# Scores turned by VectorE for batches 2 to 7, low parts of the weights by GpSimd, a new order of the first block, and four output tiles at the end

## The chip, the core and the metric

The kernel runs on one core of a Trainium2 chip. Its time is the device time of one execution in microseconds (us). A profile of another execution gives the start and length of every instruction. TensorE (PE) multiplies, VectorE (DVE) and ScalarE (ACT) work on whole tiles, GpSimd (POOL) is a fourth engine, and SyncE (SP) here only issues DMAs. Every engine works through its own queue in order and waits on semaphores for the others.

## What is computed

Attention over 8 batches, 8 heads, 576 positions and 64 columns a head, and behind it a gated layer on the 4608 x 512 result:

```python
mask_local = (rel >= 0) & (rel < stride)                      # heads 0 to 3, stride = 32
mask_strided = (rel >= 0) & (pos[None, :] % stride == pos[:, None] % stride)   # heads 4 to 7
scores = np.where(masks, scale * q @ k.T, -1e9)
attn = softmax(scores) @ v                                    # -> x, 4608 x 512
gate = 1.0 / (1.0 + np.exp(-(x @ w_gate)))                    # 512 x 1536
out = (gate * (x @ w_val)) @ w_out                            # 1536 x 512
```

## The kernel before

**The gated layer.** The 512 first positions of each batch make one block of 512 tokens (blocks 0 to 7); the 64 left over of every batch make block 8. A block goes through 12 slices of the 1536 columns. A slice f has three groups of 12 TensorE products of 128 x 512: the gate (PSUM bank `g`), the value (bank `v`) and the output, which adds to four banks in two tiles `o0` and `o1`. Twelve, because every 32-bit factor is split into a rounded high part and a low part, and three products replace one: `xh` and `xl` for the tokens, two halves of `w` for the weights, `hh` and `hl` for the hidden values. After the gate, ScalarE computes `t` and `e`; VectorE makes `e`, `t` and `hl` of them and of `v`, ScalarE `hh`. The output group of a slice comes one slice later (`last`). At a block's end the four output banks are copied to tiles `ob`, the even ones by ScalarE (buffer `ost`) and the odd ones by VectorE (buffer `l0`), and a DMA takes each out. The banks of the next block's output are free when the copies are done.

**Attention** goes by pairs of heads: steps 0 and 2 of a batch are local, 1 and 3 strided. For each pair: Q and V load, Z sets padding to zero (GpSimd), S computes scores as small products (`s`), F adds the mask and subtracts the maximum (VectorE), E takes the exponential (ScalarE), N normalises (VectorE), T turns the result with TensorE transposes into PSUM (`t`), P copies it back to SBUF (`pt`, ScalarE), X weighs the values (`x`, products of 64 x 64 array tiles), H and L split the result into `xh` and `xl`, R keeps the left-over positions. One PSUM tile of two banks, tag `a`, serves s, t and x in turn.

**Order.** In blocks 1 to 6, while block k is computed, the attention of batch k + 1 is strewn between its groups: `block` calls the next piece of the generator `attention` after the groups in `AT`, numbered 0 to 8 over three slices. For these blocks TensorE's order is the program's, and the order of the other engines is left to a scheduler. The first block, with the attention of batches 0 and 1 and the preparation of the weights, follows the string `ORDER`, for all engines: a token such as `X13` is step X of batch 1, pair 3; `W3.0` loads weight 0 of slice 3, `a`, `b` (ScalarE), `w` (VectorE), `u` (ScalarE) and `l` (VectorE) make its high and low parts; `g`, `s`, `m`, `x`, `y` and `O` are the parts of the gated layer.

Of the kernel before, what the change touches and what calls it, by code (L numbers as in the profile page):

```python
# [62 lines left out]
w1.2 g1.0.3 g1.1.3 g0.1.3 a2.2 g2.0 m0 u1.2 b2.2 l1.2 s1 W3.1 w2.2 x0 g2.1 a3.0 y0 u2.2 m1 b3.0 l2.2 s2 W3.2
w3.0 x1 O0 a3.1 y1 u3.0 m2 b3.1 l3.0 W4.0 S10 x2 w3.1 a3.2 O1 Z10 F10 Q11 u3.1 b3.2 W4.1 a4.0 w3.2 g3.0 E10
l3.1 y2 b4.0 N10 g3.1 a4.1 W4.2 u3.2 s3 l3.2 w4.0 O2 b4.1 m3 a4.2 W5.0 w4.1 x3 b4.2 T10 y3 u4.0 W5.1 w4.2 O3
P10 l4.0 u4.2 a5.0 l4.2 u4.1 g4.0 b5.0 l4.1 W5.2 w5.0 a5.1 b5.1 u5.0 g4.1 W6.0 w5.1 s4 l5.0 u5.1 l5.1 a5.2
g5.0 b5.2 m4 W6.1 w5.2 x4 a6.0 y4 u5.2 X10 b6.0 l5.2 s5 W6.2 w6.0 a6.1 O4 V11 b6.1 u6.0 W7.0 w6.1 H10 g5.1
# [14 lines left out]
def attention_then_glu(ctx, tc, qk_l, qk_s, v_l, v_s, w_all, consts, out):  # L82
# [75 lines left out]
    def lower(f, i):  # L158
        a, _ = words.pop((f, i))
        nc.vector.tensor_tensor(wl[f][i], a.bitcast(F32), wh[f][i].bitcast(F32), op=ALU.subtract)  # L160

    def pair(b, step, space):
# [88 lines left out]

        def spread():
            tp = todo["spread"]
            tiles["pt"] = pt = space.tile([P, 2 * SS * QB], F32, tag="pt", name=f"pt{b}_{step}")
            n = len(pairs) * P
            for lo, hi in ((0, BANK), (BANK, n)):
                if hi > lo:
                    nc.scalar.copy(pt[:, lo:hi], tp[:, lo:hi])  # L258
            if ns % 2:
                nc.scalar.copy(pt[:QB, n : n + P], tp[:QB, n : n + P])  # L260
# [331 lines left out]
```

## Time and profile before

| | |
|---|---|
| median of 3 runs | 1027.22 us (1026.4 to 1027.34) |
| profiled execution | 1023.94 us, span 1022.1 us |
| mean granted TensorE clock | 0.987 |
| instructions | 18250 |
| HBM read, written | 55.42 MB, 9.44 MB |

The span is the time from the first to the last instruction. A row of a group reads: line, engine, operation, what is written and from what, shape and number; behind the bar its busy us, the mean ns of one, and the idle time of the engine just before it, with what ended that. A row of a timeline reads: start in us from the span's beginning, length in us, engine, line, operation, shape and number of equal ones. PE is TensorE's products and PEld its weight loads, which overlap. A 32-bit small product shows as two entries.

### The profile page before, as it was taken

Reading aid. Unit: us, or ns where it says so; the run is one execution under the profiler, and the core shown is the slowest. Engines: PE = TensorE matmul, PEld = TensorE weight load, DVE = VectorE, ACT = ScalarE, POOL = GpSimd, SP = SyncE. Lnnn points to the kernel's source line nnn. Section 1 sums busy time; section 2 is a strip of 40 time slices with the busy share of each in tenths; the row PEclk is TensorE's granted clock in tenths of the full one; section 3 lists DMA queues with packets and bytes.
Section 4 is the critical chain, followed back from the end, with each engine's and each line's share of the span. In section 5 each row is a group of like instructions: output and inputs, shape, how many; then the busy total and the mean of one; then the engine's idle time right before and its main releaser. Section 6 shows DMA issues by size and latency. Waiting matters only on the chain.

```text
span 1022.1 us, 18250 instructions
## 1 busy us (share of the span) xinstructions
PE 995.9 (97%) x7984; PEld 812.5 (79%) x7984; DVE 491.3 (48%) x850; ACT 340.4 (33%) x683; POOL 3.4 (0%) x20
## 2 busy tenths in 40 slices
PE   4999999999999999999999999999999999999996
PEld 4787778888888888888888888888888888888885
DVE  6788864444444454444544454444444533333322
ACT  4787853322222232222222222223222322222221
POOL 0000000000000000000000000000000000000000
PEclk7899999999999999999999999999999999999999
DMA  7666632110211121101211021112110010001001
GB/s 256 210 178 214 210 97 79 51 41 28 89 40 51 40 77 55 51 22 45 82 50 37 29 91 41 51 40 71 61 51 17 1 42 1 1 0 42 1 1 42
DMA packets 19872, 66.04 MB, mean 65 GB/s; under 512 B 2256, under 2 KB 2384, under 8 KB 19792
## 3 DMA queue, kind: packets, MB, share of 16 engines
q1 hardware_dynamic: 18352, 59.28, 17.9%
q10 hardware_dynamic: 1440, 5.59, 1.7%
q8 instruction: 63, 1.03, 0.4%
q14 instruction: 17, 0.14, 0.0%
HBM read 55.42 MB, written 9.44 MB: 63 GB/s over the span
## 4 chain that ended last, share of the span: by engine, by line
PE 91%; DMA 3%; DVE 3%; ACT 2%; issue 0%; SPq 0%; ACTq 0%; DVEq 0%
PE v L359 28%; PE o L413 27%; PE g L359 27%; PE x L276 4%; PE s L206 3%; DMA raw<-in_w_all 2%; PE t L245 2%; ACT high L137 1%; PE gv L359 1%; ACT low L141 0%; DMA qk<-in_qk_l 0%; DVE high L147 0%; PE t L249 0%; DVE w L160 0%; ACT pt L258 0%
## 5 line engine op out<-in xcount | busy, mean ns | idle before, releaser
L413 PE MATMUL o<-w,hh 128*128 128x512 f32 x864 | 269.1, 393 | 0.0
L359 PE MATMUL v<-xh,w 128*128 128x512 f32 x784 | 264.8, 398 | 0.0
L359 PE MATMUL g<-xh,w 128*128 128x512 f32 x784 | 259.1, 391 | 0.0
L413 PEld LDWEIGHTS o<-w,hh 128*128 128x128 f32 x864 | 160.1, 188 | 33.3
L376 DVE TENSOR_SCALAR t<-t 128x512 int32<-128x512 int32 x96 | 41.0, 427 | 281.6 <-ACT t L373 281.6
L359 PEld LDWEIGHTS v<-xh,w 128*128 128x128 f32 x784 | 147.6, 188 | 33.1
L359 PEld LDWEIGHTS g<-xh,w 128*128 128x128 f32 x784 | 147.5, 188 | 31.0 <-issue 0.2
L413 PE MATMUL o<-w,hl 128*128 128x512 f32 x432 | 168.3, 389 | 0.0
L373 ACT ACTIVATE t<-g 128x512 f32<-128x512 f32 x96 | 57.4, 598 | 314.5 <-PE g L359 314.5
L359 PE MATMUL v<-xl,w 128*128 128x512 f32 x392 | 153.6, 392 | 0.0
L359 PE MATMUL g<-xl,w 128*128 128x512 f32 x392 | 152.8, 390 | 0.0
L400 DVE SCALAR_TENSOR_TENSOR e<-e,v 128x512 f32<-128x512 f32 x96 | 66.0, 687 | 125.5 <-PE v L359 125.5
L392 ACT ACTIVATE hh<-t 128x512 fp32r<-128x512 f32 x108 | 68.3, 632 | 148.6 <-DVE t L401 145.6
L395 DVE SCALAR_TENSOR_TENSOR hl<-t,hh 128x512 fp32r<-128x512 f32 x108 | 74.7, 691 | 48.5 <-ACT hh L392 48.5
L413 PEld LDWEIGHTS o<-w,hl 128*128 128x128 f32 x432 | 81.1, 188 | 17.4 <-DVE hl L395 0.2
L359 PEld LDWEIGHTS g<-xl,w 128*128 128x128 f32 x392 | 73.9, 188 | 15.2
L359 PEld LDWEIGHTS v<-xl,w 128*128 128x128 f32 x392 | 73.9, 189 | 13.8
L401 DVE SCALAR_TENSOR_TENSOR t<-t,e 128x512 f32<-128x512 f32 x96 | 66.4, 692 | 3.3
L374 ACT ACTIVATE e<-g 128x512 f32<-128x512 f32 x96 | 57.1, 595 | 0.0
L276 PEld LDWEIGHTS x<-pt,vv 64*64 64x64 f32 (+1 forms) x1856 | 37.0, 142 | 13.7 <-issue 9.3
L230 ACT ACTIVATE sb<-sb 128x640 f32<-128x640 f32 (+1 forms) x32 | 23.8, 745 | 70.4 <-DVE sb L226 70.4
L276 PE MATMUL x<-pt,vv 64*64 64x32 f32 (+1 forms) x1856 | 40.9, 230 | 3.3 <-DVE xl L311 1.4
(59 smaller groups left out, 675.4 us busy)
## 6 DMA issues: line engine op xcount, KB each, us to landing
raw<-in_w_all SPq DMA_DIRECT2D x36, 512.0 KB, 3.8
qk<-in_qk_s SPq DMA_DIRECT2D x14, 599.0 KB, 3.9
vv<-in_v_l SPq DMA_DIRECT2D x13, 640.0 KB, 4.1
qk<-in_qk_l SPq DMA_DIRECT2D x14, 592.0 KB, 4.0
out<-ob SPq DMA_DIRECT2D x32, 256.0 KB, 2.0
vv<-in_v_s SPq DMA_DIRECT2D x13, 384.0 KB, 3.2
vv<-in_v_l ACTq DMA_DIRECT2D x3, 640.0 KB, 5.8
qk<-in_qk_s ACTq DMA_DIRECT2D x2, 599.0 KB, 4.7
```

The lines of the kernel that those rows point to most:

```text
L206: nc.tensor.matmul(sc[g * m : (g + 1) * m, j * BANK + s * kk : j * BANK + (s + 1) * kk], qk[d, q0 : q0 + m], qk[d, k0 : k0 + kk], start=Tr ...
L230: nc.scalar.activation(prob, prob, AF.Exp, scale=SCALE)
L276: nc.tensor.matmul(xp[j * D : (j + 1) * D, r * BANK + (u * per + g) * m : r * BANK + (u * per + g + 1) * m], v[rows, (u * per + g) * P + j ...
L359: nc.tensor.matmul(o, w, x, start=first and n == 0, stop=last and n == len(todo) - 1)
L373: nc.scalar.activation(t, g, AF.Tanh, scale=0.5)
L374: nc.scalar.activation(e, g, AF.Exp)
L376: nc.vector.tensor_scalar(ti, ti, 0x7FFFFFFF, None, op0=ALU.bitwise_and)
L392: nc.scalar.activation(hh, t, AF.Copy, scale=half)
L395: nc.vector.scalar_tensor_tensor(hl, t, half, hh.bitcast(F32), op0=ALU.mult, op1=ALU.subtract)
L400: nc.vector.scalar_tensor_tensor(e, e, 1.0, v, op0=ALU.min, op1=ALU.mult)
L401: nc.vector.scalar_tensor_tensor(t, t, 1.0, e, op0=ALU.add, op1=ALU.mult)
L413: nc.tensor.matmul(acc[k][i], h[:, i * P : (i + 1) * P], w, start=f == 0 and n == 0, stop=f == NF - 1 and n == 2,)
```

## The change

- For batches 2 to 7 the steps T and P fall away. In their place stands `turn_blocks`: eight VectorE instructions a pair, each transposing the 32 x 32 blocks of 32 partitions. The values and the strided classes are laid out otherwise on the host for these batches (`by_batch`, `FEW`, `MOST`), so that the weighing finds its rows; `weigh` takes half as many groups in a row from one half of the partitions (`per`) before it goes to the other half.
- A pair now has two pieces instead of three, at slots 0 and 7 instead of 0, 4 and 6.
- `lower`, the low part of each of the 36 weights, goes from VectorE to GpSimd.
- `ORDER` is another order of the same steps.
- In block 8 the four output tiles have four buffers (`ost`, `l0`, `t`, `e`) instead of two.

```diff
+BY_PE = 2
-AT = (0, 4, 6)
+AT = (0, 7)
 ORDER = """
...
-y10 l11.1 X13 s11 a11.2 g11.1 H13 b11.2 L13 R13 w11.2 O10 m11 u11.2 l11.2 x11 y11
+l11.1 a11.2 T13 b11.2 g11.1 P13 w11.2 u11.2 l11.2 X13 m11 x11 R13 y11 H13 L13
...
+FEW, MOST = slice(0, BY_PE), slice(BY_PE, B)
...
     def lower(f, i):
         a, _ = words.pop((f, i))
-        nc.vector.tensor_tensor(wl[f][i], a.bitcast(F32), wh[f][i].bitcast(F32), op=ALU.subtract)
+        nc.gpsimd.tensor_tensor(wl[f][i], a.bitcast(F32), wh[f][i].bitcast(F32), op=ALU.subtract)
...
+        def turn_blocks():
+
+            tiles["pt"] = pt = space.tile([P, 2 * SS * QB], F32, tag="pt", name=f"pt{b}_{step}")
+            src, dst = (x[:, : 2 * ns * QB].rearrange("p (t k) -> p t k", k=QB) for x in (tiles["sb"], pt))
+            for n in range(P // LB):
+                for h in range(2):
+                    to, rows, col = (n // 2 * 2 + h) * LB, n * LB, n % 2 * LB
+                    nc.vector.transpose(dst[to : to + LB, :, col : col + LB], src[rows : rows + LB, :, h * LB : (h + 1) * LB])
...
-            per = LG if local else 2
+            per = (LG if local else 2) // (1 if b < BY_PE else 2)
...
-                    if s < ns // 2 * 2:
+                    if b >= BY_PE:
+                        at = (j * ns + u) * QB + g * LB
+                    elif s < ns // 2 * 2:
...
-            do["F"](), do["E"](), do["N"]()
-            yield
-            do["T"](bank("a", f"t{b}_{step}"))
-            do["P"]()
+            do["F"](), do["E"](), do["N"](), do["B"]()
             yield
             do["X"](bank("a", f"x{b}_{step}"))
...
-            ob = (work if i % 2 else odd).tile([P, DM], F32, tag="l0" if i % 2 else "ost", name=f"ob{k}_{i}")
+            tag = ("ost", "l0", "t", "e")[i if k == B else i % 2]
+            ob = (odd if tag == "ost" else work).tile([P, DM], F32, tag=tag, name=f"ob{k}_{i}")
```

In the rows below a number at the front of a name is the batch or block, the next the pair or slice.

TensorE in block 2, where the first local pair of batch 3 was turned, before (`v2_1` is the value of slice 1, `o2_0` the first output tile):

```order
L359 MATMUL v2_1_2891<-xh2_1792,w1_1_66 128x512
L245 MATMUL t3_0_2910<-cst_61,sb3_0_2779 128x128 x4
L249 MATMUL t3_0_2910<-cst_61,sb3_0_2779 64x64 x2
L413 MATMUL o2_0_2920<-w0_2_64,hh2_0_2843 128x512 x2
L413 MATMUL o2_0_2920<-w0_2_64,hl2_0_2844 128x512
```

and the same place now:

```order
L369 MATMUL v2_1_2896<-xh2_1792,w1_1_66 128x512
L423 MATMUL o2_0_2915<-w0_2_64,hh2_0_2848 128x512 x2
L423 MATMUL o2_0_2915<-w0_2_64,hl2_0_2849 128x512
L423 MATMUL o2_0_2915<-w0_2_64,hh2_0_2848 128x512 x2
L423 MATMUL o2_0_2915<-w0_2_64,hl2_0_2849 128x512
```

The output products follow the value's directly.

VectorE at the start of block 2, from the mask's end to the next slice, before (`ob1_1` and `ob1_3` are the copies of the second and fourth output tile of block 1):

```order
L400 SCALAR_TENSOR_TENSOR e2_0_2768<-e2_0_2768,v2_0_2830 128x512
L401 SCALAR_TENSOR_TENSOR t2_0_2769<-t2_0_2769,e2_0_2768 128x512
L234 TENSOR_REDUCE mx3_0_2780<-sb3_0_2779 128x10
L425 COPY ob1_1_2864<-o1_0_1940 128x512
L235 TENSOR_SCALAR mx3_0_2780<-mx3_0_2780 128x10
L395 SCALAR_TENSOR_TENSOR hl2_0_2844<-t2_0_2769,hh2_0_2843 128x512
L236 RECIPROCAL mx3_0_2780<-mx3_0_2780 128x10
L237 TENSOR_TENSOR sb3_0_2779<-sb3_0_2779,mx3_0_2780 128x640
L425 COPY ob1_3_2870<-o1_1_1941 128x512
L376 TENSOR_SCALAR t2_1_2887<-t2_1_2887 128x512
```

and now:

```order
L410 SCALAR_TENSOR_TENSOR e2_0_2764<-e2_0_2764,v2_0_2835 128x512
L411 SCALAR_TENSOR_TENSOR t2_0_2765<-t2_0_2765,e2_0_2764 128x512
L236 TENSOR_REDUCE mx3_0_2776<-sb3_0_2775 128x10
L436 COPY ob1_1_2869<-o1_0_1939 128x512
L237 TENSOR_SCALAR mx3_0_2776<-mx3_0_2776 128x10
L405 SCALAR_TENSOR_TENSOR hl2_0_2849<-t2_0_2765,hh2_0_2848 128x512
L238 RECIPROCAL mx3_0_2776<-mx3_0_2776 128x10
L239 TENSOR_TENSOR sb3_0_2775<-sb3_0_2775,mx3_0_2776 128x640
L261 STREAM_TRANSPOSE pt3_0_2826<-sb3_0_2775 32x10x32 x8
L436 COPY ob1_3_2875<-o1_1_1940 128x512
L386 TENSOR_SCALAR t2_1_2892<-t2_1_2892 128x512
```

The eight transposes stand ahead of the fourth output copy; blocks 3 to 6 have the same order. Block 1 has another one now (before it was that of block 2):

```order
L236 TENSOR_REDUCE mx2_0_1800<-sb2_0_1799 128x10
L237 TENSOR_SCALAR mx2_0_1800<-mx2_0_1800 128x10
L238 RECIPROCAL mx2_0_1800<-mx2_0_1800 128x10
L410 SCALAR_TENSOR_TENSOR e1_0_1787<-e1_0_1787,v1_0_1859 128x512
L239 TENSOR_TENSOR sb2_0_1799<-sb2_0_1799,mx2_0_1800 128x640
L411 SCALAR_TENSOR_TENSOR t1_0_1788<-t1_0_1788,e1_0_1787 128x512
L261 STREAM_TRANSPOSE pt2_0_1850<-sb2_0_1799 32x10x32 x8
L436 COPY ob0_1_1893<-o0_0_748 128x512
L405 SCALAR_TENSOR_TENSOR hl1_0_1873<-t1_0_1788,hh1_0_1872 128x512
L386 TENSOR_SCALAR t1_1_1916<-t1_1_1916 128x512
L436 COPY ob0_3_1899<-o0_1_749 128x512
```

There the transposes stand ahead of the second output copy as well.

TensorE at the end of the first block, where batch 1's last pair is weighed (`x1_3`), before:

```order
L359 MATMUL g0_11_1673<-xh0_101,l11_0_1616 128x512
L276 MATMUL x1_3_1697<-pt1_3_1686,vv1_3_1576 64x54 x22
L359 MATMUL v0_11_1725<-xh0_101,h11_1_1692 128x512
L359 MATMUL v0_11_1725<-xl0_102,h11_1_1692 128x512
L359 MATMUL v0_11_1725<-xh0_101,l11_1_1693 128x512
```

and now:

```order
L369 MATMUL v0_11_1712<-xh0_101,l11_1_1680 128x512
L289 MATMUL x1_3_1733<-pt1_3_1725,vv1_3_1595 64x54 x22
L369 MATMUL g1_0_1774<-xh1_585,w0_0_62 128x512
L369 MATMUL g1_0_1774<-xl1_586,w0_0_62 128x512
L369 MATMUL g1_0_1774<-xh1_585,w0_0_62 128x512
L208 MATMUL s2_0_1801<-qk2_0_1795 32x64 x40
```

Before, the value group and an output group followed `x1_3`. Now nine of the twelve products of block 1's first gate stand ahead of that pair's transposes, the value group ahead of `x1_3`, and behind it only the last three products of the gate, which need its split.

More of the change, by code (lines that the diff above doesn't have):

```diff
@@ L63 @@
[L63 to L67, printed above, removed]
@@ new lines @@
+a0.2 b1.1 L00 T02 b0.2 W2.0 w1.1 u1.0 W2.1 X01 P02 l1.0 Z03 F03 u1.1 g0.0.0 V03 l1.1 Q10 g1.0.0 R01 H01 g0.1.0
+w0.2 g1.1.0 E03 L01 a2.1 N03 u0.2 g1.0.1 b2.1 l0.2 X02 a2.0 b2.0 w2.1 W1.2 W2.2 g0.0.1 V10 w2.0 H02 T03 R02
+u2.1 L02 g1.1.1 P03 l2.1 g1.0.2 u2.0 a1.2 X03 l2.0 b1.2 W3.0 w1.2 g1.1.2 H03 g0.0.2 R03 L03 u1.2 g0.1.1 a2.2
+l1.2 g1.1.3 b2.2 g0.0.3 a3.0 W3.1 w2.2 g0.1.2 s0 g1.0.3 g0.1.3 u2.2 g2.0 b3.0 m0 l2.2 a3.1 W3.2 w3.0 s1 u3.0
+b3.1 l3.0 g2.1 x0 W4.0 w3.1 a3.2 y0 u3.1 m1 S10 b3.2 l3.1 x1 W4.1 w3.2 O0 Q11 s2 y1 u3.2 Z10 F10 a4.0 l3.2
@@ new lines @@
+b4.0 g3.0 a4.1 W4.2 w4.0 b4.1 E10 W5.0 w4.1 O1 m2 u4.1 N10 x2 l4.1 s3 g3.1 y2 a4.2 u4.0 T10 m3 b4.2 l4.0 g4.1
+x3 W5.1 w4.2 P10 y3 a5.0 u4.2 g4.0 b5.0 l4.2 W5.2 w5.0 a5.1 b5.1 u5.0 W6.0 w5.1 X10 s4 l5.0 u5.1 m4 O2 V11
+l5.1 a5.2 R10 b5.2 a6.0 W6.1 w5.2 H10 g5.1 b6.0 L10 u5.2 W6.2 w6.0 x4 l5.2 u6.0 y4 O3 a6.1 l6.0 b6.1 W7.0 w6.1
+a6.2 g5.0 b6.2 u6.1 W7.1 w6.2 l6.1 u6.2 O4 a7.0 l6.2 s5 b7.0 m5 a7.1 W7.2 w7.0 x5 S11 b7.1 y5 g6.0 u7.0 W8.0
+w7.1 Q12 l7.0 Z11 F11 u7.1 a7.2 l7.1 b7.2 g6.1 s6 W8.1 w7.2 a8.0 E11 g7.0 m6 u7.2 N11 x6 l7.2 a8.1 g7.1 s7 y6
@@ L285, in weigh @@
                 full = ns // 2 * P
-                src = xp.rearrange("p (r n) -> p r n", r=2)[:, :, :full].rearrange("p r (u n) -> p u r n", n=P)
-                main = [(src, lambda x: x[:, c, :].rearrange("p (u r n) -> p u r n", r=2, n=P))]
+                src = xp.rearrange("p (r n) -> p r n", r=2)[:, :, :full].rearrange("p r (u n) -> p u r n", n=per * LB)
+                main = [(src, lambda x: x[:, c, :].rearrange("p (u r n) -> p u r n", r=2, n=per * LB))]
                 left = [(xp[:, full : full + REST], lambda x: x)]
@@ L318, in pair @@
         return dict(
-            Q=load_qk, V=load_v, Z=room, S=score, F=soft, E=expo, N=norm, T=turn, P=spread, X=weigh, H=split_high,
+            Q=load_qk, V=load_v, Z=room, S=score, F=soft, E=expo, N=norm, T=turn, B=turn_blocks, P=spread, X=weigh, H=split_high,
             L=split_low, R=keep_rest,
@@ L534, in _layouts @@
     slot, half = np.divmod(np.arange(NG), 2)
-    first = slot % 2 * (SS // 2 * 2 * GC) + (slot // 2 * 2 + half) * GC
-    classes = first[:, None] + np.arange(GC)
+    by_slot = slot % 2 * (SS // 2 * 2 * GC) + (slot // 2 * 2 + half) * GC
+    by_half = half * (SS * GC) + slot * GC
     def grouped(a):
         a = pad(a.reshape(B, H // 2, CLS, STRIDE, D), NG * GC - STRIDE, 3)
-        return a[:, :, :, classes].transpose(0, 1, 3, 2, 4, 5).reshape(B, H // 2, NG, GS, D)
+        a = np.concatenate(
+            [a[some][:, :, :, first[:, None] + np.arange(GC)] for some, first in ((FEW, by_slot), (MOST, by_half))], 0
+        )
+        return a.transpose(0, 1, 3, 2, 4, 5).reshape(B, H // 2, NG, GS, D)
     def columns(a):
@@ L549, in stacked, with by_batch @@
         a = pad(pad(a, -n % (2 * per), 2), QB - a.shape[3], 3)
-        a = a.reshape(B, 2, 2, -1, 2, per, QB, D).transpose(0, 1, 4, 6, 3, 5, 2, 7)
-        return a.reshape(B, 2, P, -1)
+        a = a.reshape(-1, 2, 2, a.shape[2] // (2 * per), 2, per, QB, D).transpose(0, 1, 4, 6, 3, 5, 2, 7)
+        return a.reshape(-1, 2, P, a.shape[4] * per * P)
+    def by_batch(a, per, n):
+        return np.concatenate([stacked(a[FEW], per)[..., :n], stacked(a[MOST], per // 2)[..., :n]], 0)
     keys = np.arange(NBL)[:, None] * LB + np.arange(KL)[None, :]
-    v_l = stacked(np.concatenate([lead, vl], 2)[:, :, keys], LG)[..., : VL * P]
-    v_s = stacked(grouped(vs), 2)
+    v_l = by_batch(np.concatenate([lead, vl], 2)[:, :, keys], LG, VL * P)
+    v_s = by_batch(grouped(vs), 2, SS * P)
     wg, wv = (w.reshape(NC, P, NF, P).transpose(2, 1, 0, 3).reshape(NF, P, 512) for w in (w_gate, w_val))
```

19 lines of the change are left out of this document (7 added, 12 removed).

## The prediction

> **What bounds the kernel now.** I read the page's busy times, then the chain that ended last, then the stretches by stage (busy us of each engine, granted TensorE clock, DMA share).
>
> ```profile
> PE 995.9 (97%) x7984; PEld 812.5 (79%) x7984; DVE 491.3 (48%) x850; ACT 340.4 (33%) x683; POOL 3.4 (0%) x20
> PE 91%; DMA 3%; DVE 3%; ACT 2%; issue 0%; SPq 0%; ACTq 0%; DVEq 0%
> 0.00:25.00 25.00, 12.16 (x382) 10.57 (x384) 16.42 (x28) 10.29 (x18) 0.60 (x6) 0.73 0.73 259
> 25.00:50.00 25.00, 23.13 (x200) 18.23 (x195) 19.20 (x39) 18.33 (x42) 0.00 (x0) 0.79 0.65 204
> 50.00:100.00 50.00, 48.97 (x403) 39.66 (x402) 41.84 (x74) 39.11 (x66) 0.20 (x1) 1.00 0.63 197
> 200.00:300.00 100.00, 100.00 (x854) 81.40 (x853) 47.64 (x81) 27.32 (x57) 0.40 (x2) 1.00 0.17 57
> ```
>
> From 200 to 300 us TensorE is busy for all 100 us at clock 1.00, VectorE for 47.64. There time is the sum of what TensorE is given, and an instruction taken from it is worth its full place in the stream. Only the first 50 us (12.16 and 23.13 of 25) and the end hold TensorE's waits. So each part of the change is asked: does it shorten TensorE's stream, or make TensorE wait?
>
> **1. Transposes leave TensorE.** The next rows are the timeline of TensorE in block 1 round the transposes (t) of a local pair and then of a strided one (start us, length us).
>
> ```profile
> 215.94 0.39 PE L359 MATMUL v<-xh,w 128*128 128x512 f32 x1
> 218.68 0.60 PE L245 MATMUL t<-cst,sb 128*128 128x128 f32 x4
> 219.21 0.30 PE L249 MATMUL t<-cst,sb 64*64 64x64 f32 x2
> 222.28 0.39 PE L359 MATMUL g<-xh,w 128*128 128x512 f32 x1
> 241.32 0.39 PE L359 MATMUL g<-xh,w 128*128 128x512 f32 x1
> 244.04 0.39 PE L359 MATMUL v<-xh,w 128*128 128x512 f32 x1
> 246.78 0.82 PE L245 MATMUL t<-cst,sb 128*128 128x128 f32 x6
> 250.18 0.39 PE L359 MATMUL g<-xh,h 128*128 128x512 f32 x1
> ```
>
> A group of 12 products without anything between takes 244.04 - 241.32 = 2.72 us. From 215.94 to 222.28 are two such groups and the local transposes: 6.34 - 5.44 = 0.90 us with the changeovers. From 244.04 to 250.18: 6.14 - 5.44 = 0.70 us for a strided pair. A batch has two of each, 3.20 us; batches 2 to 7 give 6 x 3.20 = **-19.2 us**. The weighing products stay the same in number; their row halves only alternate twice as often, priced at nothing here (a rival below). ScalarE's copies of the turned scores go too, off the path.
>
> **2. Transposes come to VectorE.** Eight instructions a pair, 32 partitions x 320 columns (local) or 384 (strided). No row shows one. The nearest are VectorE's groups by shape:
>
> ```profile
> L311 DVE TENSOR_TENSOR xl<-x,xh 128x512 fp32r<-128x512 f32 x16 | 11.1, 691 | 13.7 <-ACT xh L307 13.7
> L311 DVE TENSOR_TENSOR xl<-x,xh 128x288 fp32r<-128x288 f32 x16 | 7.3, 458 | 10.5 <-ACT xh L307 10.5
> ```
>
> That is (691 - 458)/224 = 1.04 ns a column, so 0.49 us at 320 columns and 0.56 at 384. Low end 0.41, if each starts 0.08 before the one ahead ends, as independent instructions do below (267.65 to 268.38 is 0.73 for a length of 0.81); high end 0.82, if four-byte values go at half the rate (0.33 more). I take 0.49 and 0.56, the columns being nearest. By load they fit: 2 x 8 x (0.49 + 0.56) = 16.8 us a batch into some 52 idle us of each 100. What matters is who stands behind a burst of 8 x 0.49 = 3.9 us: at a block's start it is the copies that free the output banks. VectorE, ScalarE and TensorE there in block 2:
>
> ```profile
> 265.99 0.74 ACT L230 ACTIVATE sb<-sb 128x640 f32<-128x640 f32 x1 [2.58 <-DVE sb L226]
> 267.65 0.81 DVE L234 TENSOR_REDUCE mx<-sb 128x10 f32<-128x640 f32 x1
> 268.38 0.68 DVE L425 COPY ob<-o 128x512 f32<-128x512 f32 x1
> 269.89 0.83 DVE L237 TENSOR_TENSOR sb<-sb,mx 128x640 f32<-128x640 f32 x1
> 271.23 0.69 DVE L425 COPY ob<-o 128x512 f32<-128x512 f32 x1 [0.51 <-DMA out<-ob]
> 271.49 0.39 PE L359 MATMUL v<-xh,w 128*128 128x512 f32 x1
> ```
>
> Without the transposes the next block's output products start at 271.49 + 2.72 = 274.21 and reach the second bank pair half a group later, at 275.57. In blocks 2 to 6 the fourth output copy stands behind the burst: 269.89 + 0.83 + 0.04 + 3.92 + 0.69 = 275.37. It just fits, **0**; a stall begins at (275.57 - 271.45)/8 = 0.515 us a transpose. In block 1 the second output copy is behind the burst too, and the fourth has its buffer and waits for its DMA (268.38 to 271.23: 2.85 us from start to start). The normalising now follows the exponential at once: 265.99 + 0.74, reduce 0.81, two small ones 0.4, then e 0.7, multiply 0.83 and t 0.6 as they overlap, to 270.0; burst to 273.9; fourth copy from 276.8 to 277.5: **+1.9 us** once. Two slots further there is room: the next e starts some 3 us before its bank is wanted. The weighing comes one group later (slot 7 for 6), so at a block's end its split has the output group and nine products of the next gate, 2.72 + 9 x 0.227 = 4.8 us; three VectorE steps of 512 columns (0.69 as in the xl row) with a copy on ScalarE, begun with the weighing, and 0.8 of low parts need some 3: 0.
>
> **3. The first block.** The low part of 36 weights leaves VectorE for GpSimd, and the order is new. TensorE's waits of the whole run by releaser (us in total, times, longest), and three groups by shape:
>
> ```profile
> PE t L245 <- DVE sb L237: 6.7, 3, 5.5
> PE x L276 <- DVE xl L311: 1.4, 1, 1.4
> PE x L276 <- ACT pt L258: 1.1, 1, 1.1
> PE x L276 <- ACT pt L260: 0.8, 1, 0.8
> PE gv L359 <- DVE w L160: 0.5, 1, 0.5
> L160 DVE TENSOR_TENSOR w<-high,w 128x512 fp32r<-128x512 f32 x34 | 23.2, 687 | 6.4 <-ACT w L156 6.2
> L187 POOL MEMSET sb<- 128x120 f32 x16 | 3.2, 201 | 771.7 <-PE t L249 750.7 <-PE t L245 20.8 <-POOLq L580 0.3
> L368 ACT ACT_TABLE_LOAD x4 | 5.1, 1283 | 0.1
> ```
>
> The 5.5 is the first softmax and stays. The other waits for VectorE are 1.2 + 1.4 + 0.5 = 3.1; VectorE loses 36 x 0.687 = 24.7 us of work, so I count 2.5 of them. The two waits for pt (1.1 + 0.8 = 1.9) stand where weighing follows its transposes directly; the new order puts 12 products between. Against it: at the end of the block only three products follow batch 1's last weighing, and they need its split.
>
> ```profile
> 40.21 0.91 PE L276 MATMUL x<-pt,vv 54*64 54x54 f32 x44
> 27.33 0.37 ACT L316 COPY xr<-x 128x36 f32<-128x36 f32 x3
> 41.94 0.82 DVE L311 TENSOR_TENSOR xl<-x,xh 128x288 fp32r<-128x288 f32 x3 [0.55 <-ACT xh L307]
> ```
>
> From the weighing's end (41.12) to the low part's end (42.76) are 1.6 us, with the rest copies (0.37) ahead 2.0 idle. Sum -2.5 - 1.9 + 2.0 = **-2.4 us**; ends -4.4 (no idle at the border, all else as counted) and +2.0 (nothing gained). GpSimd's price: low end VectorE's 0.69, high end three times the memset's rate for two reads and a write, 3 x 201/120 x 512 = 2.6 us; I take 1.2, nearer the memset (0.86). 36 x 1.2 = 43 us in the 130 us of weight loading, 0.5 later each, hidden because TensorE names a weight once (0.5). Uncovered it would be up to 36 x 0.5 = 18 us. The memsets of the padding (0.2 us) now stand in GpSimd's queue between low parts; they are wanted by the normalising alone, after an exponential. The order adds two table loads on ScalarE (39.11 busy of 50), which the weights loaded ahead cover; uncovered, 2 x 1.3 us. Loads keep their number and queues. SP's own longest wait is
>
> ```profile
> SPq L127 <- ACT low L141: 75.4, 32, 5.2
> ```
>
> so a weight's load starts when ScalarE has read the raw buffer, as before; batch 0's value loads now stand behind the third weight, hidden by the first softmax.
>
> **4. Four output tiles at the end.**
>
> ```profile
> L433 SPq DMA_DIRECT2D out<-ob x8: 466/567/590, 1013.1 to 1018.7; - x8
> 1013.41 0.39 PE L413 MATMUL o<-w,hl 128*128 128x512 f32 x1
> 1016.13 0.58 ACT L427 COPY ob<-o 128x512 f32<-128x512 f32 x1 [3.08 <-DMA out<-ob]
> 1017.51 0.69 DVE L425 COPY ob<-o 128x512 f32<-128x512 f32 x1 [3.73 <-DMA out<-ob]
> ```
>
> With own buffers the third copy starts when the last product ends (1013.80) and the fourth is done by 1015.2. Then issue is the bound: 1013.1 + 7 x 0.567 = 1017.1 for the last DMA instead of 1018.7, **-1.6 us**.
>
> **Sum:** -19.2 + 1.9 - 2.4 - 1.6 = -21.3 us. The profiled execution took 1023.94 (span 1022.1): 1002.6. The median of the runs shown is 1027.22, 3.3 above it, so I forecast 1027.22 - 21.3 = 1005.9, say **1006**.
>
> **Rivals.** *Quicker weighing.* If alternating the row halves lets weight loads run ahead, the weighing nears the pace of the scores, which change halves with every product:
>
> ```profile
> 225.10 1.49 PE L276 MATMUL x<-pt,vv 64*64 64x32 f32 x72
> 234.90 0.92 PE L206 MATMUL s<-qk 64*64 64x54 f32 x48
> ```
>
> 20.7 against 19.2 ns apiece: 72 x 1.5 ns = 0.11 us in a local pair, and 44 x 1.5 = 0.07 in a strided one; 12 of each make -2.1, so 1004. [...]
>
> *Dear transposes.* At 0.8 us the fourth copy is late by 8 x (0.8 - 0.515) = 2.3 us in five blocks and block 1 loses 8 x 0.31 = 2.5 more: +14, about 1020. For it: no row shows the instruction. Against: one pass a column is what every VectorE row of this size shows.
>
> *Slower than before.* The same place, from the point at which 40 x (p - 0.515) + 8 x (p - 0.49) reaches 21.3, p = 0.95 us. At 1.1 it is 28, and the strided bursts (8 x 1.26 = 10 us) pass the 5.4 us (two groups) after which a value bank is wanted again, so 1035 and more. That needs two passes and more overhead than any row has.
>
> *GpSimd blocks VectorE.* From 50 to 100 us VectorE is busy for 41.84 of 50. Some 13.7 low parts leave (-9.4); if each keeps VectorE's two-input work waiting for its whole 1.2 us, 16.4 come back: 48.9 of 50, just fitting. At 1.6 us it is 54.4, 4.4 over in every 50, 11 us over 130 and the opening's gain gone: 1020. [...]
>
> **Chances.** As forecast 0.66; quicker weighing 0.10; dear transposes 0.10; GpSimd blocking 0.10; slower 0.04. The forecast's own range: -4.4 for the first block (-2.0 against the sum) and local transposes at 0.41 (8 x 0.08 = -0.6) give 1003; +2.0 there (+4.4) and 0.56 (block 1 +0.6, five others 8 x 0.045) give 1013. With the quicker weighing below and the nearest of the dearer cases above, 1000.5 to 1014. A change of 0.2% (2 us) is about what can be told from none. Faster 0.95, same 0.01, slower 0.04.
>
> **What would show it.** Right: no t rows on TensorE after 150 us, blocks 1 to 6 at 107.9 us instead of 111.1 with block 1 nearly 2 longer; transposes of 0.5 us; TensorE's first wait after 100 us at the block border and one for an output copy in block 1; last DMA issued 4 us after the first. Wrong: waits of output products for copies in each block (dear transposes), two-input VectorE rows longer than 0.69 or 0.83 us in the first 130 us (the lock), or a first block that ends later than before.

## The result and the profile after

| | before | after |
| --- | --- | --- |
| median of the runs (us) | 1026.81 (4 runs, 1025.0 to 1027.34) | 1010.53 (4 runs, 1007.15 to 1012.41) |
| ratio, 95% interval | | 0.9837 [0.9819, 0.9855] |
| profiled execution, its span | 1023.94, 1022.1 | 1010.32, 1008.5 |

The changed kernel is 1.6% faster: 16.3 us between the medians, 13.6 between the two profiled executions. The forecast was 21.3 (1006 us).

The page of the changed kernel first: busy time by engine, and the chain that ended last.

```profile
PE 976.4 (97%) x7840; PEld 793.5 (79%) x7840; DVE 584.4 (58%) x1006; ACT 323.8 (32%) x637; POOL 53.7 (5%) x56
PE 85%; DMA 6%; DVE 4%; ACT 4%; issue 0%; SPq 0%; ACTq 0%; DVEq 0%
```

TensorE still bounds the kernel, but DMA has 6% of the chain where it had 3, and GpSimd works for 53.7 us instead of 3.4. To see where the 13.6 us lie, I cut the span at two instructions that both kernels have: the 80 score products of block 1's first pair, which close the first block, and TensorE's last product. The rows are TensorE's timeline, first before (the last product, 1013.41 + 0.39, stands in the prediction), then after.

```profile
151.08 1.04 PE L206 MATMUL s<-qk 64*32 64x64 f32 x80
373.32 1.04 PE L206 MATMUL s<-qk 64*32 64x64 f32 x80
```

```profile
156.16 1.04 PE L208 MATMUL s<-qk 64*32 64x64 f32 x80
265.85 1.04 PE L208 MATMUL s<-qk 64*32 64x64 f32 x80
373.74 1.04 PE L208 MATMUL s<-qk 64*32 64x64 f32 x80
1001.04 0.39 PE L423 MATMUL o<-w,hl 128*128 128x512 f32 x1
```

| part | before | after | change | forecast |
| --- | --- | --- | --- | --- |
| to the score products of block 1 | 151.08 | 156.16 | +5.1 | -2.4 |
| from there to the last product's end | 862.72 | 845.27 | -17.4 | -17.3 (-19.2 + 1.9) |
| from there to the end of the span | 8.3 | 7.1 | -1.2 | -1.6 |

The stream came out as worked out, and the tail nearly; the first block grew where it should have shrunk. Of the stream: block 1 lasts 265.85 - 156.16 = 109.69 us and block 2 lasts 107.89, for the forecast's 107.9 with block 1 nearly 2 longer. The transposes on VectorE, by shape:

```profile
L261 DVE STREAM_TRANSPOSE pt<-sb 32x384 f32<-32x384 f32 x96 | 54.7, 570 | 1.5
L261 DVE STREAM_TRANSPOSE pt<-sb 32x320 f32<-32x320 f32 x96 | 48.3, 503 | 1.5
```

570 and 503 ns, where the columns of other rows gave 560 and 490. Block 2's start shows the narrow margin that the prediction worked out (a stall from 0.515 us a transpose). VectorE's burst, the fourth output copy behind it, and the product that needs the bank which that copy frees:

```profile
274.41 4.12 DVE L261 STREAM_TRANSPOSE pt<-sb 32x320 f32<-32x320 f32 x8
277.97 0.61 PE L423 MATMUL o<-w,hh 128*128 128x512 f32 x2
278.56 0.69 DVE L436 COPY ob<-o 128x512 f32<-128x512 f32 x1
279.33 0.71 PE L423 MATMUL o<-w,hh 128*128 128x512 f32 x2
```

The copy ends at 279.25, and the product starts at 279.33: it fits, at a cost of 0.1 us in that group. In block 1 the second copy stands behind the burst too, and the fourth waits for its buffer's DMA:

```profile
163.66 4.11 DVE L261 STREAM_TRANSPOSE pt<-sb 32x320 f32<-32x320 f32 x8
167.80 0.69 DVE L436 COPY ob<-o 128x512 f32<-128x512 f32 x1
168.64 0.70 PE L423 MATMUL o<-w,hh 128*128 128x512 f32 x2 [0.19 <-DVE ob L436]
170.61 0.69 DVE L436 COPY ob<-o 128x512 f32<-128x512 f32 x1 [0.24 <-DMA out<-ob]
171.45 0.70 PE L423 MATMUL o<-w,hh 128*128 128x512 f32 x2 [0.98 <-DVE ob L436]
```

From the last value product ahead of these output products to the gate's first behind them are 172.91 - 168.06 = 4.85 us, in block 2 280.80 - 277.75 = 3.05: this is block 1's whole loss.

At the end the two last copies wait for no DMA any more, and the last DMA is issued 4.4 us after the first:

```profile
1001.47 0.59 ACT L438 COPY ob<-o 128x512 f32<-128x512 f32 x1 [0.81 <-PE o L423]
1002.09 0.69 DVE L436 COPY ob<-o 128x512 f32<-128x512 f32 x1 [0.70 <-ACT ob L438]
L444 SPq DMA_DIRECT2D out<-ob x8: 543/562/596, 1000.7 to 1005.1; - x8
```

Now the first block. Two things stand out in its timeline. The first had no place in the sum: some VectorE instructions that start while GpSimd works on a low part are longer than they ever were.

```profile
90.70 1.29 POOL L162 TENSOR_TENSOR w<-high,w 128x512 fp32r<-128x512 f32 x1 [3.56 <-ACT w L158]
90.74 1.79 DVE L149 CUSTOM_DVE_ANT_0 high<-high,low 128x1024 uint16<-128x1024 uint16 x1
...
99.27 1.29 POOL L162 TENSOR_TENSOR w<-high,w 128x512 fp32r<-128x512 f32 x1 [4.72 <-ACT w L158]
...
99.58 1.01 DVE L237 TENSOR_SCALAR mx<-mx 128x12 f32<-128x12 f32 x1
...
100.89 0.83 DVE L239 TENSOR_TENSOR sb<-sb,mx 128x648 f32<-128x648 f32 x1
101.87 0.85 PE L247 MATMUL t<-cst,sb 128*128 128x128 f32 x6 [1.29 <-DVE sb L239]
```

The joining of the words (0.69 us elsewhere) starts at 90.74 and ends at 92.53, which is GpSimd's end (91.99) and 0.54 more. The step over 12 columns (0.17 elsewhere) starts at 99.58 and ends at 100.59, as GpSimd ends (100.56). TensorE's wait of 1.29 us behind it holds those 0.84. The second is the border of the first block, where the prediction counted 2.0 us of idle time: it is 1.44 and 0.36.

```profile
152.30 0.91 PE L289 MATMUL x<-pt,vv 54*64 54x54 f32 x44
154.65 0.50 PE L369 MATMUL g<-xh,w 128*128 128x512 f32 x1 [1.44 <-ACT xh L320]
155.50 0.50 PE L369 MATMUL g<-xl,w 128*128 128x512 f32 x1 [0.36 <-DVE xl L324]
```

TensorE's waits of the whole run by releaser (us in total, times, longest) show more: the wait for the normalising was 6.7 us before, and the waits of a gate for ScalarE and of a value group for a low part on GpSimd are new.

```profile
PE t L247 <- DVE sb L239: 9.4, 4, 4.8
PE g L369 <- ACT e L378: 2.3, 2, 1.5
PE v L369 <- POOL w L162: 0.9, 1, 0.9
```

Over the whole first block TensorE idles 23.9 us (156.16 less 132.26 busy) where it idled 17.9 (151.08 less 133.22). So the 5.1 us are all waiting, and the granted clock has no part in them: in the first 30 us it was 0.72 before and 1.00 after.

So two theories. L: GpSimd's low parts hold up VectorE, and the softmaxes and weights come late. O: the new order itself loses the time. They were put to the test one at a time and together.

### The profile page after: what moved, and what is told of

Read it like the earlier page. It is cut to its first block, busy times and chain, and to the rows that moved or that the text cites. A ratio compares the mean times of both kernels' runs of the same rounds, so it can differ in the third digit from the quotient of the medians.

```text
span 1008.5 us, 18125 instructions
## 1 busy us (share of the span) xinstructions
PE 976.4 (97%) x7840; PEld 793.5 (79%) x7840; DVE 584.4 (58%) x1006; ACT 323.8 (32%) x637; POOL 53.7 (5%) x56
## 4 chain that ended last, share of the span: by engine, by line
PE 85%; DMA 6%; DVE 4%; ACT 4%; issue 0%; SPq 0%; ACTq 0%; DVEq 0%
PE o L423 27%; PE v L369 26%; PE g L369 26%; DMA raw<-in_w_all 5%; PE x L289 3%; PE s L208 2%; ACT high L139 1%; ACT low L143 1%; DVE sb L228 1%; DVE sb L239 0%; DVE high L149 0%; DVE mx L227 0%; DMA qk<-in_qk_l 0%; DVE pt L261 0%; DVE mx L236 0%
## 5 line engine op out<-in xcount | busy, mean ns | idle before, releaser
L369 PE MATMUL v<-xh,w 128*128 128x512 f32 x784 | 261.4, 394 | 1.1 <-POOL w L162 0.9
L261 DVE STREAM_TRANSPOSE pt<-sb 32x320 f32<-32x320 f32 (+1 forms) x192 | 103.0, 536 | 3.1
L423 PEld LDWEIGHTS o<-w,hl 128*128 128x128 f32 x432 | 81.1, 188 | 17.9 <-DVE hl L405 0.6
L369 PEld LDWEIGHTS g<-xl,w 128*128 128x128 f32 x392 | 73.7, 188 | 15.8 <-DVE xl L324 0.7
L162 POOL TENSOR_TENSOR w<-high,w 128x512 fp32r<-128x512 f32 x34 | 46.2, 1369 | 93.6 <-ACT w L158 93.6
L289 PEld LDWEIGHTS x<-pt,vv 64*64 64x64 f32 (+1 forms) x1856 | 34.4, 139 | 12.0 <-issue 10.4
```

The source lines that it names most:

```text
L162: nc.gpsimd.tensor_tensor(wl[f][i], a.bitcast(F32), wh[f][i].bitcast(F32), op=ALU.subtract)
L261: nc.vector.transpose(dst[to : to + LB, :, col : col + LB], src[rows : rows + LB, :, h * LB : (h + 1) * LB])
L289: nc.tensor.matmul(xp[j * D : (j + 1) * D, r * BANK + (u * per + g) * m : r * BANK + (u * per + g + 1) * m], v[rows, (u * per + g) * P + j ...
L369: nc.tensor.matmul(o, w, x, start=first and n == 0, stop=last and n == len(todo) - 1)
L423: nc.tensor.matmul(acc[k][i], h[:, i * P : (i + 1) * P], w, start=f == 0 and n == 0, stop=f == NF - 1 and n == 2,)
```

## The experiments

The time of a kernel's first block differs by several us from one execution to the next: its end is at 156.16 and 152.51 us in two profiles of the changed kernel, at 154.44 and 149.94 in two of e6's. So each verdict below rests on medians of runs made side by side, and on what the profiles show alike. e7, e8 and e9 were executed once each. The three groups with intervals stood beside medians of before of 1023.95, 1027.37 and 1027.22.

| | order | low parts | output copies | median (runs) | ratio to before, 95% |
| --- | --- | --- | --- | --- | --- |
| e1 | new | VectorE | as changed | 1008.91 (5) | 0.9842 [0.9819, 0.9865] |
| e2 | old | GpSimd | as changed | 1011.06 (6) | 0.9865 [0.9842, 0.9888] |
| e3 | old | VectorE | as changed | 1007.07 (5) | 0.9815 [0.9789, 0.9842] |
| e4 | new | GpSimd, halves | as changed | 1009.3 (5) | 0.9848 [0.9820, 0.9875] |
| e5 (the change) | new | GpSimd | as changed | 1011.54 (5) | 0.9849 [0.9825, 0.9872] |
| e6 | old | VectorE | ScalarE | 1004.0 (5) | 0.9766 [0.9744, 0.9788] |
| e10 | new | VectorE | ScalarE | 1008.19 (6) | 0.9822 [0.9798, 0.9847] |
| e11 | new | GpSimd | ScalarE | 1008.36 (6) | 0.9815 [0.9789, 0.9841] |
| e12 (e6 again) | old | VectorE | ScalarE | 1002.23 (5) | 0.9767 [0.9743, 0.9792] |

**e1: low parts back on VectorE**

```diff
-        nc.gpsimd.tensor_tensor(wl[f][i], a.bitcast(F32), ...)
+        nc.vector.tensor_tensor(wl[f][i], a.bitcast(F32), ...)
```

> The changed kernel with the 36 low parts back on VectorE; the new order of the first block, the turning by VectorE and the four tiles at the end stay. Theory L (GpSimd's low part holds up VectorE instructions that start beside it): VectorE's shift of the high words is back at 0.42 us (mean 0.598 now), its joining step at 0.69 (0.790), and the score products of block 1 (80 of them) start 2 to 4 us earlier than the 156.2 us of the changed kernel; about 1007 us. Theory O (the new order itself costs the 5 us): the 1.8 us of idle at the border and the waits before it stay, and VectorE has 24.7 us more to do in an order that places it elsewhere: 156 us or later, 1010.5 to 1013.

**e2: the old order, low parts on GpSimd**

```diff
-C Q00 Q01 W0.0 S00 Z00 F00 S01 a0.0 Q03 ...
+C Q00 Q01 V00 W0.1 S00 Z00 F00 S01 Q03 ...
```

> The changed kernel with the old order of the first block; the low parts stay on GpSimd. Theory L: VectorE's rows are as long as in the changed kernel (0.6 and 0.79 us), block 1's score products start at 154 to 157 us, 1008 to 1012 us. Theory O: they start at 151 us as before, 1005 to 1006 us.

**e3: both edits of e1 and e2**

> The changed kernel with both undone: old order, low parts on VectorE; what is left is the turning by VectorE and the four tiles at the end. Both theories: first block as in the kernel before (score products of block 1 at 151 us), then 17.5 us less of TensorE's stream and 1.2 us less at the end: 18.7 us under the kernel before, 1008 us against its median of 1026.8 (1005.3 against its profiled run).

VectorE's shift and joining step in the first block, in the changed kernel, in e1 and in e2 (groups by shape: busy us, mean ns):

```profile
L149 DVE CUSTOM_DVE_ANT_0 high<-high,low 128x1024 uint16<-128x1024 uint16 x36 | 28.4, 790 | 7.5 <-ACT low L143 3.4
L148 DVE TENSOR_SCALAR high<-high 128x512 int32<-128x512 int32 x36 | 21.5, 598 | 6.9 <-ACT high L139 6.8
```

```profile
L149 DVE CUSTOM_DVE_ANT_0 high<-high,low 128x1024 uint16<-128x1024 uint16 x36 | 24.9, 692 | 6.0 <-ACT low L143 1.8
L148 DVE TENSOR_SCALAR high<-high 128x512 int32<-128x512 int32 x36 | 15.2, 422 | 4.5 <-ACT high L139 4.2
```

```profile
L149 DVE CUSTOM_DVE_ANT_0 high<-high,low 128x1024 uint16<-128x1024 uint16 x36 | 33.0, 917 | 8.2 <-ACT low L143 4.2
L148 DVE TENSOR_SCALAR high<-high 128x512 int32<-128x512 int32 x36 | 20.1, 558 | 5.3 <-ACT high L139 5.2
```

The rows grow with the low parts on GpSimd in either order, and in e1 they are back. Of the 24.5 us that leave VectorE in the first block, these two groups alone give 9.8 back in the changed kernel and 13.0 in e2. With smaller groups (the low part of the hidden values, the small steps of the softmaxes) it is some 17 us in the changed kernel: VectorE is relieved of 7 us and not of 24.5.

In time, the three stand in the order e3, e1, e2: every run of e1 (1008.0 and more) lies above every run of e3 (1007.69 and less), and every run of e2 (1009.28 and more) above e1's. With the old order, the median with GpSimd is 1011.06 - 1007.07 = 4.0 us higher: theory L, against O's 1005 to 1006 for e2. With the low parts on VectorE, the median with the new order is 1.8 higher, and the idle border stays in e1 (1.4 and 0.3 us): theory O has a share that L denied. And e3, with neither, comes near what was expected of it: 16.9 us under before, for 18.7.

This is likely and not proved. The interval of e1 overlaps with both others, those of e2 and e3 meet at 0.9842, and e8 below, whose first block is e3's, took 1011.58 us. Nor do the profiles say that all 4.0 us are waits for VectorE. The first block ends at 156.39 us in e2 and at 150.59 in e3; 2.4 of these 5.8 us are TensorE's idle time (20.6 for 18.2), and 3.4 its busy time for the same products: the granted clock was 0.50 in e2 from 34 to 38 and from 106 to 108 us, in e3 only from 100 to 102. Whether GpSimd's work brings that about is open; e8, whose first block has none, had three such stretches.

**e4: the low part in two instructions**

```diff
+        for lo in (0, DM // 2):
+            cut = slice(lo, lo + DM // 2)
+            nc.gpsimd.tensor_tensor(wl[f][i][:, cut], ...)
```

> The changed kernel with each low part on GpSimd in two instructions of 256 columns. Theory L: a VectorE instruction that starts beside one waits at most half as long: the longest joining step falls from 1.79 to about 1.3 us, the shortest steps (12 columns) from 1.02 to about 0.6, and block 1's score products start 1 to 2 us earlier, about 1009 us. If the low part's own length (1.37 us for VectorE's 0.69) were what costs, two instructions are no shorter together: 156 us or later, 1010.5 to 1012.

The joining step's durations (shortest, median, longest ns) in the changed kernel, and in e4:

```profile
L149 DVE CUSTOM_DVE_ANT_0 high<-high,low x36: 691/693/1799, 16.4 to 146.7; 128x1024 uint16<-128x1024 uint16 x36
```

```profile
L149 DVE CUSTOM_DVE_ANT_0 high<-high,low x36: 691/693/1243, 17.2 to 143.1; 128x1024 uint16<-128x1024 uint16 x36
```

The longest falls by 0.56 us (1.3 us expected): what it has above 0.69 goes from 1.11 to 0.55, while GpSimd's mean goes from 1369 ns to 845; the longest of the small steps fell from 1.02 to 0.61. In time e4 cannot be told from the changed kernel: 1009.3 against 1010.5 and 1011.5, the intervals overlap. Its first block ended at 152.4 us, 3.8 earlier for 1 to 2 expected, but e5 shows that the changed kernel itself can end it as early.

**e5: the changed kernel again**

> The changed kernel itself, timed on this chip beside the kernel before, since the four runs so far stood beside a before of 1023.95 us and not of 1026.8. Theory L and O alike: the profile's first block stays long (score products of block 1 at 155 to 157 us). If the low parts on GpSimd cost some 3 us whatever the order (L), its median stands 2 to 4 us above the version with both undone (1007.07) and within 1.5 us of the one with the old order alone (1011.06).

1011.54, 15.8 us under its before: within half a microsecond of the first result's 16.3. By ratio it stands 3.5 us above e3 and 1.6 below e2, with intervals that overlap. Its profile's first block ended at 152.5 us where 155 to 157 was expected of it, a miss; the executions' spread is as large as what is looked for, and one profile's first block decides nothing.

**e6: all output copies but the last block's on ScalarE** (on e3)

```diff
-            if i % 2:
+            if i % 2 and k == B:
                 nc.vector.tensor_copy(ob, o)
```

> The version with old order and low parts on VectorE, and all four output copies of a block on ScalarE (but at the end). If the extra 1.8 us of block 1 is the second and fourth copy behind the eight transposes, block 1 falls from 109.4 to 107.8 us from score products to score products and TensorE's waits for an output copy (1.2 us, 2) vanish; blocks 2 to 6 fall by 0.1 each (the output group beside the fourth copy from 2.83 to 2.72). In all 2 us under that version: 1005. If it is the third and fourth copy waiting for their buffers' DMA, block 1 keeps 1 us or more of it.

Block 1 by the score products of e6:

```profile
154.44 1.04 PE L208 MATMUL s<-qk 64*32 64x64 f32 x80
262.12 1.04 PE L208 MATMUL s<-qk 64*32 64x64 f32 x80
```

107.68 us for block 1 and, on average, for those behind it; TensorE waits for no output copy. But it waited for none in e3 either, which had lost only 0.25 us in block 1 (107.93), not 1.8: the 109.4 expected of it was near the changed kernel's 109.69. The reordering of the first block had changed what the scheduler put in VectorE's queue in block 1 (with the old order, the second copy stands ahead of the burst). So the 1.8 us belongs to the new order: block 1 takes 109.94 us in e1, and 107.94 and 107.93 in e2 and e3. e6 is below e3 by ratio (0.9766 and 0.9815, intervals that just part), by 5 us and not by the 2 expected. The profiles show some 1.5 of them, about 0.25 in each of blocks 1 to 6; the rest stays open.

**e7: the weighing one group earlier**

```diff
-AT = (0, 7)
+AT = (0, 6)
```

> The changed kernel with the weighing one group earlier (slot 6 for 7), so behind the gate's products as in the kernel before. If the local pair's weighing is quicker (1.29 us for 72 products, 1.42 before) because the row halves alternate from product to product, it stays at 1.29. If it is quicker because of the group it follows, it is 1.42 again. The blocks 2 to 6 stay at 107.9 us either way within 0.3, since the transposes are done some 2 us before the earlier slot.

```profile
282.02 1.35 PE L289 MATMUL x<-pt,vv 64*64 64x32 f32 x72
283.31 0.50 PE L369 MATMUL v<-xh,w 128*128 128x512 f32 x1
```

Behind the gate's products as before, the local weighing takes 283.31 - 282.02 = 1.29 us and not 1.42: the slot doesn't make it quicker. What is left is the new layout, in which the row half changes after every four products and not every eight. That this alternation is the cause is argued and not shown: it came with other addresses, and the strided pairs, whose row half also changes twice as often, stayed at 0.84. Block 2 stayed at 107.88 us as expected; the one execution took 1008.79.

**e8: GpSimd work beside VectorE's regular steps** (on e3; k is the block, B is 8)

```diff
-        high(), low()
+        high()
+        for n in range(2 * (k > B - 2)):
...
+            if k == B - 1:
+                nc.gpsimd.tensor_tensor(junk, hh.bitcast(F32), wl[0][n].bitcast(F32), op=ALU.subtract)
+            else:
+                nc.gpsimd.tensor_copy(junk, hh.bitcast(F32))
+        low()
```

> The version with old order and low parts on VectorE, with GpSimd work added in blocks 7 and 8 alone, where VectorE runs five regular steps for each tile of hidden values: after each high part two subtractions of 128x512 in block 7, two copies of 128x512 in block 8, into tiles that nobody reads. Theory L: in block 7 the steps with two SBUF inputs (0.69 us) and the one that clears the sign (0.43 us) take up to 1.3 us longer when they start beside GpSimd, while the step with one input from PSUM (0.69) stays; the low part, which starts with GpSimd's, is the one that is hit. In block 8 it tells whether a GpSimd copy does the same. If GpSimd's work does not hold VectorE up, all rows stay at 0.43 and 0.69. TensorE waits for nothing new in either (slack of two groups): the time stays within 0.2%.

Block 7 of e8, VectorE's low part and GpSimd's subtraction:

```profile
L405 DVE SCALAR_TENSOR_TENSOR hl<-t,hh 128x512 fp32r<-128x512 f32 x10 | 6.9, 692 | 7.5 <-ACT hh L402 7.5
L416 POOL TENSOR_TENSOR junk<-hh,w 128x512 f32<-128x512 f32 x20 | 30.0, 1518 | 51.4 <-ACT hh L402 51.4
```

A miss: VectorE stayed at 692 ns, and GpSimd's mean grew to 1518 from the 1290 of its undisturbed rows (1.29 us in the first block's timeline above). Both waited for the same high part, and VectorE was first by 0.1 us (852.43 and 852.54 in one slice). So here it was GpSimd's row, the one that started second, that grew. TensorE waited for nothing in blocks 7 and 8, as expected, but the time (1011.58, one run) missed by far: the first block, where nothing was changed, ended at 159.1 us with three stretches at half clock (around 36, 108 and 137 us).

**e9: the same, with GpSimd already at work** (on e3)

```diff
         high(), low()
+        for n in range({B - 1: 5, B: 8}.get(k, 0)):
...
+            if k == B - 1:
+                nc.gpsimd.tensor_tensor(junk, hl.bitcast(F32), wl[0][0].bitcast(F32), op=ALU.subtract)
+            else:
+                nc.gpsimd.tensor_copy(junk, hl.bitcast(F32))
```

> As the run with GpSimd work in blocks 7 and 8, but GpSimd starts after VectorE's low part and is still at work when VectorE's next steps start: five subtractions of 128x512 for each tile of hidden values in block 7, eight copies of 128x512 in block 8, into a tile that nobody reads. By the regular times of that run the clearing of the sign (0.43 us) starts in the third subtraction and the second product step (0.69, two SBUF inputs) in the fifth; the first product step (0.69, one input from PSUM) starts beside them too. Theory L (VectorE's two-input SBUF steps and the fast one-input step wait for the running GpSimd instruction to end): in block 7 the sign step's row grows to 0.8 to 1.7 us and the second product step's by up to 1.3, the first product step stays at 0.69. [...] No lock: all rows stay.

GpSimd's group in block 7, then VectorE's (busy us, mean ns):

```profile
L416 POOL TENSOR_TENSOR junk<-hl,w 128x512 f32<-128x512 f32 x53 | 72.8, 1373 | 13.8 <-DVE hl L405 10.5
L411 DVE SCALAR_TENSOR_TENSOR t<-t,e 128x512 f32<-128x512 f32 x10 | 10.3, 1032 | 0.3
L386 DVE TENSOR_SCALAR t<-t 128x512 int32<-128x512 int32 x11 | 8.6, 783 | 28.8 <-ACT t L383 28.8
L410 DVE SCALAR_TENSOR_TENSOR e<-e,v 128x512 f32<-128x512 f32 x10 | 6.9, 687 | 13.4 <-PE v L369 13.4
```

The sign step goes from 428 to 783 ns and the step with two inputs in SBUF from 693 to 1032, while the one that reads PSUM and one SBUF tile stays at 687 beside the same GpSimd work. Beside copies in block 8 the sign step took 591 ns. Here GpSimd was at work first (in one slice from 841.23 us, the sign step from 841.80) and VectorE's rows grew by some 0.35 us, GpSimd's by 0.08 (1373 for 1290); in e8 VectorE was first and only GpSimd's grew. TensorE waited for none of it in blocks 7 and 8, and the time, 1005.26 us in one run, lies among e3's (1003.1 to 1007.69): there, where TensorE did not wait for VectorE, the longer rows cost nothing that shows.

**e10, e11, e12: order and low parts again, with the copies on ScalarE** (e10 is e1, e11 is the changed kernel, each with the edit of e6; e12 is e6)

> New order, low parts on VectorE, output copies on ScalarE. The new order costs 2.0 us in block 1 (109.94 us with it, 107.93 with the old one, low parts on VectorE in both), which the copies on ScalarE take away. If that is all that the order costs, this is within 1.5 us of the old order with the same copies (1004.0, run again beside it). If the 1.8 us of idle at the border of the first block count too, it is 2 us or more above it.

> The changed kernel with the output copies on ScalarE: new order, low parts on GpSimd. Blocks 1 to 6 at 107.7 us, so 3 us under the changed kernel (1011.2 over its nine runs): 1008. Theory L: it stays 2 to 4 us above the same kernel with low parts on VectorE. If the low parts on GpSimd cost nothing in the order that was made with them, the two are equal within 1 us.

> The fastest version so far (old order, low parts on VectorE, turning by VectorE, four tiles at the end, output copies on ScalarE) again, beside the two others: 1004 us, 22 to 24 us under the kernel before.

By the medians the new order costs 1008.19 - 1002.23 = 6.0 us, so block 1 is not all of its cost: no run of e10 (1007.21 and more) is as low as any of e12 (1004.7 and less), and the intervals part. The low parts on GpSimd cost 0.2 in that order: e11 equals e10, and the 2 to 4 us that theory L gave fell. e12 is 25.0 us under before, for 22 to 24 expected. Where the order loses is seen in the last stretch of the first block (from 120 us to block 1's score products: length, TensorE busy, and so on; the clock is third from the end). Before, after, e12, e10:

```profile
120.00:151.08 31.08, 30.08 (x287) 24.00 (x285) 22.83 (x42) 19.34 (x38) 0.20 (x1) 1.00 0.41 136
```

```profile
120.00:156.16 36.16, 32.81 (x294) 25.84 (x294) 23.80 (x38) 23.78 (x42) 9.48 (x8) 1.00 0.42 131
```

```profile
120.00:149.94 29.94, 28.95 (x280) 22.94 (x278) 21.36 (x39) 18.26 (x35) 0.20 (x1) 1.00 0.39 127
```

```profile
120.00:156.94 36.94, 33.20 (x294) 25.43 (x292) 25.42 (x45) 23.79 (x42) 0.20 (x1) 1.00 0.42 129
```

TensorE idles 1.0 us there with the old order (30.59 - 29.59 in e3 too; 1.6 in e2) and 3.0 to 3.9 with the new one, GpSimd or not (3.94 in e1; only e4, with its halves, had 2.0): the border's 1.8 us and what comes ahead of it. Over the whole first block TensorE idles 23.9 us in e10 and 18.8 in e12, so 2.75 of the 5.1 us lie in this stretch and the rest ahead of it. In block 1, e10 still lost 1.55 us (266.17 - 156.94 = 109.23 for 107.68), though the copies were on ScalarE. Its windows from 156 us tell why (the clock is third from the end):

```profile
156.00:158.00 2.00, 1.73 (x79) 1.35 (x82) 0.54 (x3) 0.93 (x2) 0.00 (x0) 0.71 0.49 202
158.00:160.00 2.00, 2.00 (x30) 1.54 (x16) 1.61 (x3) 1.55 (x2) 0.00 (x0) 0.50 0.36 80
160.00:162.00 2.00, 2.00 (x9) 1.60 (x9) 1.10 (x3) 0.74 (x1) 0.00 (x0) 0.93 0.60 235
```

After the idle border the granted clock falls to 0.50 for some 3.5 us (from the means of the three windows 1.2 + 2.0 + 0.3). e4, e5, e7 and e11 show the same between 152 and 160 us (0.50 or 0.51 in one window of 2 us each); the changed kernel's first profile and e1 do not (1.00 in each window). So the same border, 1.4 us and 0.3 to 0.4 of idle time, is followed by half clock in some executions and not in others; why was not shown. With the old order no profile had it at the border. But all seven (before, e2, e3, e6, e8, e9, e12) had such a stretch elsewhere in the first block, before the longest (0.50 from 12 to 28 and from 34 to 38 us). So half clock is no cost of the new order alone.

## Why the prediction held in sum and failed in the first block

- **Transposes off TensorE (-19.2): right.** Block 2 lost 111.11 (262.21 to 373.32) - 107.89 = 3.22 us, for 3.20 a batch. Two things cancel in it: the local weighing is 0.13 us quicker, twice a batch (the rival "quicker weighing", right in size for local pairs and wrong for strided ones), and the output groups by the burst give back 0.2 a batch, which e6 recovers (107.68).
- **Eight transposes at 0.49 and 0.56 us: right** (0.503, 0.570). "Dear transposes" and "slower" fell with them, and the margin was as narrow as worked out: of the 0.2 us nothing was left, since the group behind the fourth copy paid 0.1.
- **Block 1 (+1.9): right in size** (109.69 against 107.9), and by the steps given. What the prediction did not see is that the new order of the first block causes it, by what it makes of VectorE's queue in block 1: with the old order block 1 took 107.93 (e3).
- **Tail (-1.6): -1.2.** The third and fourth copies went as worked out; the DMAs were issued 0.63 us apart (4.4 us for seven) and not 0.567.
- **First block (-2.4): wrong.** This is the step that failed. Between the profiled executions it is +5.1; by the medians it is what is left of -16.3 beside -17.4 and -1.2, about +2.4. Of the waits that I took away (2.5 and 1.9), those for a split (1.4), for pt (1.9) and for a weight (0.5) did vanish. But others came in their place: for ScalarE's gate (2.3 us, 2.6 in e1), for a low part on GpSimd (0.9), and longer ones for the normalising (9.4 for 6.7; 9.2 in e1); that for the split at the border (1.4 + 0.4) came as counted. e1 has its low parts on VectorE, so the gate's wait, and waits of this size for the normalising, come with the new order alone. Counting only waits that exist misjudged this stretch: the sum took it that all other waits stay as they are. Two signs that the prediction named for being wrong were there, VectorE rows over 0.69 us in the first 130 us and a first block that ends later. That the total still came near is owed to the transposes, nine tenths of the sum, and supports nothing that was said of the first block.
- **GpSimd's low part at 1.2 us, hidden: 1.37, and not hidden from VectorE.** The rival that GpSimd blocks VectorE (the lock, among the signs) was right that VectorE's two-input rows grow beside GpSimd's (693 to 1032 ns in e9) and wrong in the consequence. It was priced as capacity (48.9 of 50 us, "just fitting"), and VectorE's load did fall; what came late was single short steps of a softmax. Nor was the low part hidden from TensorE, which waited 0.9 us for one at 119 us. In time, by the medians, the low parts on GpSimd cost 4.0 us with the old order, some of it perhaps the half clock, and nothing that could be told with the new one. Why the new order takes it is not settled; the order's own loss may cover it.

How large the new order's own cost is stays open between 1.8 us (e1 over e3) and 6.0 (e10 over e12); that it costs is what both pairs of runs say, the second with intervals that part.

The version with the old order, the low parts on VectorE, the turning on VectorE, four tiles at the end and the output copies on ScalarE (e6, e12) beats both kernels: 0.9766 [0.9744, 0.9788] and 0.9767 [0.9743, 0.9792] of before, against 0.9849 [0.9825, 0.9872] for the changed kernel in e6's company.

## What to carry to other kernels

Where an engine's stream is the bound, the gaps between its instructions price a removal well (3.20 us a batch forecast, 3.22 measured, with two deviations of some 0.2 that cancel). A new order of a stretch full of waits has to be priced as a new chain, not as a list of old waits removed, and with what it does to the queues behind it. Work that is moved to GpSimd to relieve VectorE should be checked for the VectorE steps that start beside it: here those with two inputs in SBUF (1032 ns for 693 in e9) and the one-input sign step (783 for 428) took longer beside GpSimd's subtractions, so what counts is who stands behind those steps, not the load.

## What the runs showed of the hardware

- Beside GpSimd's subtractions of 128x512 VectorE's two-input SBUF step took 1032 ns for 693, its sign step 783 for 428, and the PSUM-reading one 687, as in the kernel before (e9); when VectorE was first by 0.1 us, its step stayed at 692 and GpSimd's grew (1518 for 1290, e8).
- In the changed kernel a VectorE step over 12 columns that started beside a low part on GpSimd took 1.01 us for 0.17, 0.84 more; a joining step over 1024 columns took 1.79 for 0.69, 1.10 more.
- 72 weighing products took 1.29 us instead of 1.42 once the row half changed with every other block of keys and the layout with it (e7); 44 strided ones stayed at 0.84 with the same kind of change.
- An idle border of 1.8 us was followed by 3.5 us at half clock in five of seven profiles with it. All seven profiles with the old order had a stretch at half clock elsewhere in their first 112 us.
